# A fixed issue order by a table, and seven half-size products in every token tile from the fifth on

## The chip, the cores and the metric

The kernel runs on one core of one Trainium2 chip. The metric is the device time of one execution in microseconds (us). A core has five engines that run side by side, each through its own queue in order: TensorE (PE: matmul; PEld: its weight loads), VectorE (DVE), ScalarE (ACT), GpSimd (POOL) and SyncE (SP). SP and POOL issue the transfers here, which 16 DMA engines carry out. SBUF is the memory beside the engines; PSUM holds the sums of matmuls in eight banks.

## The reference

Two layers, the second fed by the first. Input x is 8 batches of 3008 rows of 256 numbers.

```
X  = rfft(x, axis=1)
Yr = Xr @ w_r - Xi @ w_i + b_r ;  Yi = Xr @ w_i + Xi @ w_r + b_i
Y  = soft_threshold(Yr, 0.01) + 1j * soft_threshold(Yi, 0.01)
y  = irfft(Y, n=3008, axis=1)              # 24064 rows of 256
h  = y @ w_in                              # 256 -> 2048
g  = s * relu(h)**2 + b
out = g @ w_out                            # 2048 -> 256
```

## The kernel before

**Spectral part.** 3008 = 94 x 32, and the transform is done in two stages of matmuls. Per batch: first stage (`s1_units`: matmul of x with A_t, a copy out of PSUM into u, transfer u to a DRAM buffer ud, and back as us, rows regrouped), then `s23_units`: second stage (F_t), mixing with w_r and w_i by three products (xf, W_t, W_g, the sum s), soft threshold (`shrink`: max, min, subtract on VectorE in a ring of buffers), four transfers ring to ring per step that regroup partitions, first inverse stage (T_t, copied to v), transfer v to DRAM vd and back as vs; then `s4_units`: last stage (C_t), copied to yt. The first batch runs by itself in `first_batch` with all banks; the other seven run beside the second layer of the batch ahead.

**Second layer.** The 24064 tokens make 48 token tiles (`_tile_order`): 12 "wide" ones of batches 0 and 1 (512 or 480 tokens), 30 "main" ones and 6 "tail" ones (512 or 384). Each tile has 16 slots (MC = 16 blocks of 128 of the 2048 inner columns). In a slot, `first_mm` does two matmuls of up to 512 columns into one half of a double bank psh; every second slot, relu (L879, psh to rt) and the square (L889 or L892, rt to gt) follow. In the slots of the next tile, the products gt x w_out of this tile run:

- plain (`second_mms`, L930 on): 4 groups of 16 matmuls of 256 columns into psa, two exits by VectorE (L954, psa to ost) and four stores;
- by sevens (`seven_mms`): the tile's gt as a 2 x 2 matrix of blocks, and w_out likewise, multiplied by seven products of half-size blocks instead of eight (Strassen-Winograd), 7 x 2 x 8 = 112 matmuls of 128 columns. The sums of blocks of gt are made on VectorE (`s_op`, L990, three of 1024 columns for each half of the inner columns) and, the fourth of them, by an accumulating DMA gt to gt that POOL issues (L983). The sums of w_out are made once (`make_t`). The seven results leave four banks in four groups (`leave`, L1023 and L1042: zz and ost), nine VectorE instructions in all. A bank psa is one of two; product four (n = 3) needs the bank of the first two.

Before, `seven` (L1087) picks 21 of the 48 tiles: three around the change of batch 0 to 1, the two ahead of each later batch, the first of most batches, and most of the last batch.

**What sets the order.** A plan written out by hand (`schedule`, `plan`) says in which slot each spectral unit is emitted. The engine of a copy or a square is chosen by a running sum of costs (`act_first`, `work`). The tile framework's scheduler then sets each engine's order by priorities; `urgent()` (L183) raises those of instructions that empty a bank.

Of the kernel before, what the change touches and what calls it, by code (L numbers as in the profile page):

```python
# [9 lines left out]
F16 = mybir.dt.float16  # L10
# [9 lines left out]
VSCALE = 1.0 / 64.0  # L20

# [75 lines left out]
def kernel(  # L97
# [70 lines left out]
    lean = [0.0]  # L168

    pe = {"on": False, "now": 0.0}  # L170

    def matmul(out, lhs, rhs, **how):
        if pe["on"]:
            pe["now"] += 0.0025 + int(np.prod(rhs.shape[1:])) / 2400.0
        return nc.tensor.matmul(out, lhs, rhs, **how)  # L175

    def work(engine, us):
        load[engine] = max(load[engine], pe["now"]) + us

    def act_first(ready, ta, td):  # L180
        return max(load["act"], ready) + ta <= max(load["dve"], ready) + td + lean[0]

    def urgent():  # L183

        return tc.high_priority(offset=200) if pe["on"] else nullcontext()

    def evac(dst, src, cols):
        ta, td = over["act"] + cols / 1200.0, over["dve"] + cols / 960.0
        with urgent():
            if act_first(pe["now"], ta, td):  # L190
                work("act", ta)
                return None, nc.scalar.copy(out=dst, in_=src)  # L192
            work("dve", td)
            return nc.vector.tensor_copy(out=dst, in_=src), None
# [3 lines left out]
    def mix_bank():  # L198
        return pools["m"].tile([P, 512], F32, name="psm", tag="psm")
# [10 lines left out]
    def two_banks():  # L210
        return pools["h"].tile([P, 2, 512], F32, name="psh", tag="psh")

    def one_bank():
        return fpool.tile([P, 512], F32, name="psf", tag="psf")
# [4 lines left out]
    def other_bank():  # L219
        return apool.tile([P, 512], F32, name="psa", tag="psa")  # L220
# [6 lines left out]
    def emit_load_x(b, first=None, chunks=range(N2 // XCH)):  # L227
        xv = x[b].rearrange("(n1 n2) d -> n1 (n2 d)", n2=N2)
        for c in chunks:
# [4 lines left out]
            if first is not None:  # L234
                gate = nc.gpsimd.tensor_copy(out=t[0:1, 0:1], in_=first)
# [133 lines left out]
    last_square = [None]  # L369
# [4 lines left out]
    def make_t(i):  # L374

        if not T_s:
            nc.vector.tensor_tensor(
                out=b_21, in0=bias_bc[:, P:D], in1=bias_bc[:, 0:P], op=ALU.subtract
            )
            T_s.append(x2pool.tile([P, 4, MC // 2, P], F16, name="T_s", tag="x2"))  # L380
        t = T_s[0]
        a, b, op = (
            (w_block(0, 1), w_block(0, 0), ALU.subtract),
            (t[:, 0], w_block(1, 1), ALU.subtract),
            (w_block(1, 1), w_block(0, 1), ALU.subtract),
            (w_block(1, 0), t[:, 1], ALU.add),
        )[i]
        with tc.issue_after(last_square[0].ins):
            nc.vector.tensor_tensor(out=t[:, i], in0=a, in1=b, op=op)
        work("dve", 0.61)  # L390
# [9 lines left out]
    def make_bias():  # L400
# [3 lines left out]
        nc.scalar.activation(out=bias_bc, in_=ps[:, 0:D], func=AF.Copy, scale=bb_bc)  # L404
# [3 lines left out]
    ring = []  # L408
    yts = {}
    tails = {}  # L410
# [3 lines left out]
    def first_batch():  # L414
# [121 lines left out]

        def turn(ec, n):

            ps = mix_bank() if ec == 0 else any_bank() if n < HW else one_bank()
            for j in range(4):  # L540
# [5 lines left out]
            evac(  # L546
                vs[(0, h)][:, k : k + 4, ec * P : (ec + 1) * P],
# [5 lines left out]
        def last_dft(ec, n):  # L553
# [5 lines left out]
            else:  # L559
                ps = other_bank() if n % 8 else one_bank()  # L560
            for j in range(4):
# [6 lines left out]
            evac(  # L568
                yt[:, ec, n : n + 4, :],
                ps[:, 0:384].rearrange("p (j n) -> p j n", n=96), 384,  # L570
            )

# [51 lines left out]
    def s1_units(b, more_banks=False):  # L624

        ud = dpool.tile([96, N2, D], F16, name="ud", tag="ud")
        hold = {}

        def unit(i):
# [4 lines left out]
            ps = any_bank() if more_banks else one_bank()  # L634
            matmul(
# [4 lines left out]
            evac(u[0:96, k : k + 2, :], ps[0:96, :].rearrange("p (j d) -> p j d", j=2), 512)  # L640
            if k == UCH - 2:
                n = 2 * i + 2
                nc.sync.dma_start(out=ud[:, n - UCH : n, :], in_=u[0:96])

        def take_rows(which=range(4)):
            uv = ud.rearrange("k n d -> (k n) d").rearrange("(q p) d -> p q d", p=P)
            for q in which:
                t = uspool.tile([P, 6, D], F16, name="us", tag="us")
                nc.sync.dma_start(out=t, in_=uv[:, 6 * q : 6 * q + 6, :])
                us[(b, q)] = t  # L650
# [3 lines left out]
    def s23_units(b):  # L654
# [6 lines left out]
        hold = {}  # L661

        def fwd_unit(i):
# [3 lines left out]
            t = us[(b, i // 3)]  # L667
            for j in range(2):
# [7 lines left out]
            evac(xt[:, 1:3].rearrange("p r c k -> p (r c k)"), bank, 512)  # L676
            nc.vector.tensor_tensor(out=xt[:, 0], in0=xt[:, 1], in1=xt[:, 2], op=ALU.add)  # L677
            work("dve", 0.34)
            xf[i] = xt

        def sum_unit(h):

            ps = one_bank().rearrange("p (i e) -> p i e", i=2)
# [6 lines left out]
            s = mpool.tile([P, 2, D], F32, name="s", tag="m")  # L690
            with urgent():
                nc.scalar.copy(out=s, in_=ps)
            work("act", 0.49)
            hold[h] = s

        def mix_unit(i):
            ps = one_bank().rearrange("p (r e) -> p r e", r=2)
            xt = xf.pop(i)
            for r in range(2):
# [5 lines left out]
            with urgent():  # L705
                nc.vector.tensor_tensor(  # L706
                    out=ring[0][:, i % 4], in0=ps,
                    in1=hold[i // 2][:, i % 2].unsqueeze(1).to_broadcast([P, 2, D]), op=ALU.add,
                )
            work("dve", 0.67)  # L710
# [5 lines left out]
        def shrink(i, n):  # L716
# [4 lines left out]
            nc.vector.tensor_tensor(out=m, in0=t, in1=lo, op=ALU.max)  # L721
            nc.vector.tensor_tensor(out=m, in0=m, in1=hi, op=ALU.min)
            nc.vector.tensor_tensor(out=t, in0=t, in1=m, op=ALU.subtract)
            work("dve", 0.21 + 0.8 * n)
            for k in range(i, i + n):
                z = ring[0][:, 6 + k % 6]
                for j in range(2):
                    for r in range(2):
                        o = z[64 * r : 64 * r + 64, j]
                        a = t[64 * j : 64 * j + 64, k - i, r]  # L730
                        if k < H - 2:
                            nc.sync.dma_start(out=o, in_=a)
                        else:
                            nc.vector.tensor_copy(out=o, in_=a)
                            work("dve", 0.13)
                zt[k] = z

        def inv_unit(i):
            ps = one_bank().rearrange("p (j e) -> p j e", j=2)
            z = zt.pop(i)  # L740
            for j in range(2):
# [7 lines left out]
            evac(v[:, h : h + 2, :], ps, 512)  # L749
            if i % 2 == 1:  # L750
                nc.sync.dma_start(
                    out=vd[2 * i - 2 : 2 * i + 2].rearrange("q p e -> p q e"), in_=v
                )
            if i == H - 1:
                hold["vv"] = vd.rearrange("q (k n) e -> (q k) (n e)", n=N2)
# [4 lines left out]
        def take_half(h):  # L760
            t = vspool.tile([96, HW, D], F16, name="vs", tag="vs")
            nc.sync.dma_start(
                out=t.rearrange("k n e -> k (n e)"),
                in_=hold["vv"][:, h * HW * D : (h + 1) * HW * D],
            )
            vs[(b, h)] = t
# [17 lines left out]
    def s4_units(b):  # L784
# [6 lines left out]
        def unit(g):  # L791
# [4 lines left out]
            ps = one_bank()  # L796
            for j in range(w):
# [6 lines left out]
            evac(  # L804
                yt[:, ec, n2 : n2 + w, 0:N1],
                ps[:, 0 : w * N1].rearrange("p (j n) -> p j n", n=N1), w * N1,
            )
            if g == len(groups) - 1 and b >= 2:
# [3 lines left out]
                nc.gpsimd.tensor_copy(out=tails[pr][:, :, half], in_=yt[:, :, :, 80:94])  # L812
# [22 lines left out]
    hold_h = {}  # L835

# [21 lines left out]
    def first_mm(ti, mc):  # L858
# [4 lines left out]
        ps = hold_h["ps"]  # L863
        for dc in range(DC):
# [12 lines left out]
        rt = rpool.tile([P, 2, 512], F32, name="rt", tag="rt")  # L877
        with urgent():
            nc.scalar.activation(out=rt[:, :, 0:w], in_=ps[:, :, 0:w], func=AF.Relu)  # L879
# [4 lines left out]
        rr = rt[:, :, 0:w]  # L884
        if halves(ti):
            rr = rr.rearrange("p k (i t) -> p k i t", i=2)
        work("act", 0.07 + w / 600.0)
        if act_first(pe["now"], 0.09 + w / 600.0, 0.07 + w / 480.0):
            nc.scalar.activation(out=gt, in_=rr, func=AF.Square)  # L889
            work("act", 0.09 + w / 600.0)  # L890
        else:
            last_square[0] = nc.vector.tensor_tensor(out=gt, in0=rr, in1=rr, op=ALU.mult)  # L892
            work("dve", 0.07 + w / 480.0)
    def store(tl, sub, src):
        kind, b, j, w = tl
        if kind == "wide":
# [3 lines left out]
            nc.sync.dma_start(  # L900
                out=rows[n2 : n2 + 4, lo : lo + w], in_=src[0 : 4 * w]
            )
            return
        if kind == "main":
            rows = out[b * N + 512 * j : b * N + 512 * (j + 1), :]
            rows = rows.rearrange("(n1 n2) d -> n2 n1 d", n2=N2)[8 * sub : 8 * sub + 8]
            nc.sync.dma_start(out=rows, in_=src)
# [4 lines left out]
        while i < end:  # L912
# [14 lines left out]
            nc.sync.dma_start(out=dst, in_=src[i - i0 : i - i0 + cnt])  # L927
            i += cnt

    def second_mms(ti):  # L930
# [6 lines left out]
        def mm(sub, mc):  # L937
# [3 lines left out]
            if h == 0 and mc == 0:  # L941
                hold["ps"] = sum_bank(ti).rearrange("p (h e) -> p h e", h=2)
            ps = hold["ps"]
            matmul(
# [5 lines left out]
            if mc == MC - 1 and (alone or h == 1 or sub == nsub - 1):  # L950
                k = h + 1
                ost = opool.tile([P, 2, D], F32, name="ost", tag="ost")
                with urgent():
                    nc.vector.scalar_tensor_tensor(  # L954
                        out=ost[0:size, 0:k], in0=ps[0:size, 0:k], scalar=s_bc[0:size],
# [3 lines left out]
                work("dve", 0.13 + 0.27 * k)  # L959
                for i in range(k):  # L960
                    store(tl, sub - k + 1 + i, ost[:, i, :])
# [7 lines left out]
    sums = {}  # L969

# [4 lines left out]
    def s_op(ti, n, q):  # L975

        size = 2 * sub_size(tiles[ti])
        if n == 1:
# [213 lines left out]
```

## Time and profile before

| | |
|---|---|
| median of 3 runs | 836.48 us (836.18 to 836.76) |
| the profiled execution | 837.46 us, its span 835.7 us |
| TensorE busy | 820.7 us, 7662 matmuls |
| ScalarE busy | 723.0 us |
| VectorE busy | 703.9 us |
| GpSimd busy | 86.3 us |
| HBM read and written | 53.52 and 46.66 MB |
| granted TensorE clock | 1.0 |

The span goes from the first to the last instruction. A busy time is the union of an engine's instructions. A row of a group gives the engine, the operation, output and input by the program's names, shapes and count, then busy time and the mean of one instruction. A matmul row's end is modelled and holds the drain, which the next matmul overlaps; so the distance between two starts says what one costs. In rows in order of time, merged rows (x7) go from the first start to the last end, and a bracket gives the idle time ahead and who ended it.

The token tiles start at 46.3 us (tile 0), 114.6 (tile 4), 302.2 (tile 15), 351.7 (tile 18), 405.5 (tile 21), 797.0 (tile 46) and 810.1 (tile 47).

### The profile page before, as it was taken

What the parts mean: (1) busy time and instruction counts of PE and PEld (TensorE: products, weight loads), DVE (VectorE), ACT (ScalarE), POOL (GpSimd) and SP (SyncE); (2) the same over time, 40 slices, a digit from 0 to 9 for tenths busy, and PEclk for the clock granted to TensorE, in tenths of its full rate; (3) what the DMA queues carried; (4) which work ended last, traced back from release to release, by engine and by line L of the source; (5) the groups of instructions that cost most, each with busy time, mean ns of one, the idle gap of its engine ahead of it and who ended that gap; (6) DMA issues with size and microseconds to landing.
All of it is one profiled execution on the core that took longest, in us unless ns stands there. A gap on an engine that the chain in (4) does not pass through costs nothing.

```text
span 835.7 us, 19552 instructions
## 1 busy us (share of the span) xinstructions
PE 820.7 (98%) x7662; PEld 598.5 (72%) x7662; DVE 703.9 (84%) x1104; ACT 723.0 (87%) x962; POOL 86.3 (10%) x114
## 2 busy tenths in 40 slices
PE   7999999999999999999999999999999999999997
PEld 6857767777677767777677776777767777767765
DVE  5988979978898888987889888797888988879785
ACT  5998988998899988998899988989879988788882
POOL 4550001100011001100011000100001000001000
PEclk9999999999999999999999999999999999999999
DMA  8954578346773378445773458724565233513321
GB/s 201 178 155 102 116 193 208 61 97 138 193 185 66 96 182 200 124 104 137 182 191 71 97 137 208 183 48 114 128 178 141 59 103 100 135 45 77 77 62 59
DMA packets 116670, 107.17 MB, mean 128 GB/s; under 512 B 12774, under 2 KB 100842, under 8 KB 115234
## 3 DMA queue, kind: packets, MB, share of 16 engines
q1 hardware_dynamic: 102498, 80.55, 34.0%
q0 software_dynamic: 14080, 25.37, 19.1%
q8 instruction: 60, 0.98, 0.5%
q14 instruction: 32, 0.26, 0.1%
HBM read 53.52 MB, written 46.66 MB: 120 GB/s over the span
## 4 chain that ended last, share of the span: by engine, by line
PE 78%; DVE 9%; ACT 5%; DMA 5%; issue 2%; POOL 0%; SPq 0%; DVEq 0%; POOLq 0%
PE psh L175 32%; PE psa L175 28%; PE psf L175 17%; ACT rt L879 2%; DVE gt L892 2%; DMA vd<-v 1%; DMA ring<-ring 1%; DMA x<-in_x_dram 1%; DVE ring L706 1%; DVE gt L990 1%; PE psm L175 1%; DVE ost L1023 1%; DMA vs<-vd 1%; ACT gt L889 1%; DVE s L990 1%
## 5 line engine op out<-in xcount | busy, mean ns | idle before, releaser
L879 ACT ACTIVATE rt<-psh 128x1024 f32<-128x1024 f32 (+2 forms) x384 | 386.9, 1009 | 56.0 <-PE psh L175 54.0
L175 PEld LDWEIGHTS <-gt 128*128 128x128 f16 (+1 forms) x3696 | 304.9, 101 | 167.2 <-issue 0.5
L175 PE MATMUL psh<-yt,w_in 128*128 128x512 f16 (+1 forms) x1344 | 396.7, 378 | 0.1
L892 DVE TENSOR_TENSOR gt<-rt 128x1024 f16<-128x1024 f32 (+2 forms) x239 | 286.0, 1201 | 81.3 <-ACT rt L879 80.6
L175 PE MATMUL psa<-w_out_t,gt 128*128 128x256 f16 (+3 forms) x2448 | 310.3, 253 | 0.0
L175 PEld LDWEIGHTS <-w_in 128*128 128x128 f16 x1536 | 136.5, 98 | 25.4 <-issue 2.9
L889 ACT ACTIVATE gt<-rt 128x1024 f16<-128x1024 f32 (+2 forms) x145 | 150.8, 1040 | 3.4
L175 PE MATMUL psa<-T_s,gt 128*128 128x128 f16 (+1 forms) x944 | 79.4, 219 | 0.0
L983 POOL DMA_DIRECT2D gt<-gt x42 | 38.0, 905 | 325.7 <-PE psh L175 87.3
L192 ACT CAST u<-psf 96x512 f16<-96x512 f32 x96 | 55.7, 582 | 9.1 <-PE psf L175 8.4
L706 DVE TENSOR_TENSOR ring<-psf,s 128x512 f16<-128x512 f32 x84 | 57.4, 684 | 4.1 <-PE psf L175 3.1
L192 ACT CAST v<-psf 128x512 f16<-128x512 f32 x79 | 45.8, 583 | 14.0 <-PE psf L175 13.5
L175 PE MATMUL psh<-tail,w_in 128*128 128x512 f16 (+1 forms) x192 | 52.1, 352 | 0.0
L239 POOL DMA_DIRECT2D x<-in_x_dram x36 | 19.2, 538 | 315.6 <-PE psf L175 314.4
L175 PEld LDWEIGHTS <-xf 128*128 128x128 f16 x504 | 46.7, 98 | 5.8 <-DVE xf L677 0.4
L175 PE MATMUL psf<-W_g,xf 128*128 128x256 f16 x336 | 50.4, 272 | 0.0
L192 ACT CAST yt<-psf 128x470 f16<-128x470 f32 (+2 forms) x84 | 43.1, 535 | 3.4 <-PE psf L175 2.2
L1023 DVE SCALAR_TENSOR_TENSOR ost<-psa,s_bc,zz 128x256 f32<-128x256 f32 (+1 forms) x80 | 34.7, 477 | 7.9 <-PE psa L175 6.4
L954 DVE SCALAR_TENSOR_TENSOR ost<-psa,s_bc,bias_bc 128x512 f32<-128x512 f32 (+2 forms) x51 | 37.1, 727 | 4.8 <-PE psa L175 2.6
L192 ACT CAST xf<-psf 128x512 f16<-128x512 f32 x64 | 37.5, 586 | 3.8 <-PE psf L175 3.7
L175 PE MATMUL psf<-x,A_t 94*96 94x512 f16 x102 | 39.0, 382 | 1.0 <-ACT yt L192 0.3
L175 PE MATMUL psf<-C_t,vs 96*128 96x94 f16 (+1 forms) x484 | 38.0, 205 | 0.1
(118 smaller groups left out, 797.0 us busy)
## 6 DMA issues: line engine op xcount, KB each, us to landing
out_dram<-ost SPq DMA_DIRECT2D x152, 128.0 KB
ud<-u SPq DMA_DIRECT2D x56, 192.0 KB
us<-ud SPq DMA_DIRECT2D x28, 384.0 KB
vd<-v SPq DMA_DIRECT2D x42, 256.0 KB
vs<-vd SPq DMA_DIRECT2D x14, 768.0 KB
x<-in_x_dram POOLq DMA_DIRECT2D x28, 376.0 KB, 6.3
gt<-gt POOLq DMA_DIRECT2D x38, 256.0 KB, 4.2
ring<-ring SPq DMA_DIRECT2D x280, 32.0 KB
```

The lines of the kernel that those rows point to most:

```text
L175: return nc.tensor.matmul(out, lhs, rhs, **how)
L192: return None, nc.scalar.copy(out=dst, in_=src)
L239: nc.gpsimd.dma_start(out=t[0:N1, i * w : (i + 1) * w], in_=xv[:, c * XCH * D + i * w : c * XCH * D + (i + 1) * w],)
L706: nc.vector.tensor_tensor(out=ring[0][:, i % 4], in0=ps, in1=hold[i // 2][:, i % 2].unsqueeze(1).to_broadcast([P, 2, D]), op=ALU.add,)
L879: nc.scalar.activation(out=rt[:, :, 0:w], in_=ps[:, :, 0:w], func=AF.Relu)
L889: nc.scalar.activation(out=gt, in_=rr, func=AF.Square)
L892: last_square[0] = nc.vector.tensor_tensor(out=gt, in0=rr, in1=rr, op=ALU.mult)
L954: nc.vector.scalar_tensor_tensor(out=ost[0:size, 0:k], in0=ps[0:size, 0:k], scalar=s_bc[0:size], in1=bias_bc[0:size].unsqueeze(1).to_broad ...
L983: nc.gpsimd.dma_start(out=a12, in_=a11, accum_op=ALU.add)
L990: nc.vector.tensor_tensor(out=out, in0=a, in1=b, op=op)
L1023: nc.vector.scalar_tensor_tensor(out=out, in0=of, scalar=s_bc[0:size], in1=other, op0=ALU.mult, op1=ALU.add)
```

## The change

- Every token tile from tile 4 to tile 45 that has 512 or 480 tokens is done by seven products: 39 tiles instead of 21.
- After the first batch, all instructions of ScalarE, VectorE, SP and POOL are recorded as pieces (`later`) and issued in a fixed order with a fixed engine, by a table of base-36 numbers (`TURNS`): piece k is issued at place k + delay, on the engine that the table names, as soon as TensorE's program reaches it (`pump`, called ahead of each matmul). The framework's own scheduling is switched off for all five engines (`manual_schedule`).
- Copies out of PSUM, relus, squares and the copy of s may go to either engine; relu gets a VectorE form.
- Two ring transfers become one where two steps are shrunk together; the load of the fourth chunk of x is planned some slots earlier; the output and rt buffers are three fixed ones used in turn.
- Asserts (`need`, `begin`) at build time, no instructions: every piece is issued behind those that it needs.

```diff
     def seven(ti):
-        if ti >= len(tiles) - 2 or not halves(ti):
-            return False
-        firsts = [mark[b] // MC for b in range(2, B)]
-        return (
-            ti >= firsts[-1] or 4 <= ti < 7 or any(m - 2 <= ti < m for m in firsts)
-            or late(ti)
-        )
+        return 4 <= ti < len(tiles) - 2 and halves(ti)
...
+    def plan_turns():
+        at = [divmod(int(TURNS[k : k + 2], 36), 4) for k in range(0, len(TURNS), 2)]
+        queue.extend(
+            (k, ("act", "dve", "sp", "pool")[at[k][1]])
+            for k in sorted(range(len(at)), key=lambda k: k + at[k][0])
+        )
+
+    def begin(op, engine):
+        assert engine in op.cost and all(n.gone for n in op.needs)
+        op.gone = True
+        op.emit(engine)
+
+    def pump():
+        while queue and queue[0][0] < len(pieces):
+            k, engine = queue.pop(0)
+            begin(pieces[k], engine)
...
     def matmul(out, lhs, rhs, **how):
-        if pe["on"]:
-            pe["now"] += 0.0025 + int(np.prod(rhs.shape[1:])) / 2400.0
+        pump()
         return nc.tensor.matmul(out, lhs, rhs, **how)
...
+        def relu(e):
+            if e == "act":
+                nc.scalar.activation(out=rt, in_=ps[:, :, 0:w], func=AF.Relu)
+            else:
+                nc.vector.tensor_scalar(
+                    out=rt, in0=ps[:, :, 0:w], scalar1=0.0, scalar2=None, op0=ALU.max
+                )
...
+        first = later(
+            relu, {"act": 0.065 + w / 600.0, "dve": 0.065 + w / 480.0},
+            needs=squares[-len(rts) :][:1] if len(squares) >= len(rts) else [], frees=ps,
+        )
...
-        first = ((0, 1, 0), (1, 3, 0)) if late(ti) else ()
-        for at, n, q in (
-            *first, (2, 2, 0), (2, 1, 1), (2, 4, 0), (3, 3, 1), (4, 2, 1), (5, 4, 1)
-        ):
-            at += alone and at > 3
-            slots[at].append(lambda n=n, q=q: s_op(ti, n, q))
+        slots[0].insert(0, lambda: own_sums(ti, 1))
+        for at, q in ((2, 0), (4 + alone, 1)):
+            slots[at].append(lambda q=q: s_op(ti, 2, q))
...
-            for c, at in enumerate((10, 14, 26, 54)):
+            free_at = 37 + 4 * (mark[b] - s1 - 50) // 16
+            for c, at in enumerate((10, 14, 26, free_at)):
...
+    osts = [opool.tile([P, 2, D], F32, name="ost", tag="ost") for _ in range(3)]
+    rts = [rpool.tile([P, 2, 512], F32, name="rt", tag="rt") for _ in range(3)]
+    ctx.enter_context(tc.manual_schedule(engines={
+        mybir.EngineType.PE, mybir.EngineType.Activation, mybir.EngineType.DVE,
+        mybir.EngineType.SP, mybir.EngineType.Pool,
+    }))
```

## The prediction, made before the changed kernel ran

> **What bounds the kernel now.** I read the page first, parts 1 and 4, then the stretches of each token tile, the waits of TensorE, and the rows in order of time at three places.
>
> ```profile
> span 835.7 us, 19552 instructions
> PE 820.7 (98%) x7662; PEld 598.5 (72%) x7662; DVE 703.9 (84%) x1104; ACT 723.0 (87%) x962; POOL 86.3 (10%) x114
> PE 78%; DVE 9%; ACT 5%; DMA 5%; issue 2%; POOL 0%; SPq 0%; DVEq 0%; POOLq 0%
> ```
>
> TensorE is the bound: it idles 15 us of 835.7. Of this, 5.4 lie in the first 46.3 us and 4.4 in the last 25.6 us, both outside the change; 5.2 lie in the token tiles between (PE busy 758.61 of 763.80). So time can be won by less TensorE work, and by at most about 5 us of idle time besides. A busy matmul row holds a drain that the next one overlaps, so true stalls are somewhat longer than this idle time.
>
> The price of a matmul is its distance to the next, not its duration. Two rows in order of time, late in the run, then two stretches of one token tile each:
>
> ```profile
> 797.38 0.55 PE L175 MATMUL psf<-w_out_t,gt 128*128 128x128 f16 x7
> 810.54 0.60 PE L175 MATMUL psf<-w_out_t,gt 128*128 128x256 f16 x4
> ...
> 797.00:810.10 13.10, 13.10 (x146) 9.32 (x144) 12.48 (x17) 10.62 (x11) 1.71 (x2) 1.00 0.30 61
> 810.11:824.00 13.89, 13.89 (x99) 9.40 (x97) 10.01 (x11) 9.60 (x11) 0.00 (x0) 1.00 0.19 58
> ```
>
> The columns of the last two are stretch, its length, then busy time and count of PE, PEld, DVE, ACT, POOL, clock, DMA share. Seven half-size matmuls take 0.55 us, the last lasting 0.219: (0.55-0.219)/6 = 0.055 us each. Four full ones: (0.60-0.272)/3 = 0.109. The first stretch runs 32 wide matmuls and one tile's seven products, the second the same 32 and one tile's plain second product.
>
> **The change, part by part.** *TensorE.* A plain tile has 4 x 16 = 64 matmuls of 256 columns: 64 x 0.109 = 6.98 us. Seven products are 7 x 2 x 8 = 112 matmuls of 128: 112 x 0.0557 = 6.24. That is 0.74 less per tile; the two stretches say 0.79. Tiles by sevens go from 21 to 39 of 48, 18 more (16 of 512 tokens, two of 480 with the same columns): **-13.4 us**. The built order has 18 x 48 = 864 more matmuls, so the change does do this. TensorE's order is now that of the program: from tile 3 on it is the same but for two matmuls in tile 12; five first-stage matmuls of batch 1 that ran in gaps ahead of tile 0 now stand inside it: 0 to 5 x 0.22 = +1.1 us, taken as 0, since the gaps ahead of it wait for copies that these five also waited for.
>
> *VectorE and ScalarE.* Each added tile brings VectorE six sums (687 ns, rows of L990) and nine exits (seven of 477, one of 413, one of 746 ns) for two exits of 748: 4.12+4.50-1.50 = 7.1 us, 128 us for 18. Against that the built order moves 121 squares from VectorE (239 to 118) to ScalarE, 39 relus to VectorE and 80 copies to VectorE. ScalarE: squares +126.9, relus -39.0, copies -46.1, together +42, 723 to 765 us. VectorE: -145.9 squares, +46.3 relus (no row; 1.22 us each, as the square of the same 1024 floats takes; at the least 0.69 as a sum of 1024 halves, 21 us less in all; at the most 1.37 as two PSUM casts of 512, 6 us more), +53.8 copies, +128: 786 us. As rows of one line overlap (three exits in 1.26 us are 0.39 apart, not 0.477), 231 more instructions cost some 0.085 less each: 766. Both engines stay below 822 as a whole, at 93 to 96%. They lie beside TensorE, and cost nothing as long as nothing waits.
>
> The dense tiles decide that. Three consecutive tiles that are plain now, with spectral work beside them:
>
> ```profile
> 351.70:405.50 53.80, 53.15 (x452) 38.06 (x450) 45.36 (x75) 48.96 (x65) 2.80 (x4) 1.00 0.51 122
> ```
>
> VectorE plus ScalarE: 94.3 us in 2 x 53.8. Two and a half added tiles (the first exits already run there) at 6.0 (7.1 less 13 x 0.085) are +15, less about 3 for squares on the cheaper engine: 106 against 2 x 51.6 = 103. Without the overlapped 0.09 of each of about 175 instructions it is 91. So between 88% and 103% of the two engines; at the upper end each such group lacks (106-103)/2 = 1.6 us, and there are six: 0 to +10 us. I take +2, nearer the lower end, because in the neighbouring tile of 17.5 us ScalarE is busy 16.67 with TensorE's idle time all from one VectorE wait (next).
>
> *The fixed order.* The only regular wait of TensorE in these tiles is this:
>
> ```profile
> PE psa L175 <- DVE ost L1023: 3.5, 7, 0.8
> PEld L175 <- DVE ost L1023: 5.1, 9, 0.9
> ...
> 358.04 0.48 DVE L1023 SCALAR_TENSOR_TENSOR zz<-psa,s_bc,bias_bc 128x256 f32<-128x256 f32 x1
> 358.43 0.68 DVE L722 TENSOR_TENSOR ring<-ring,high 128x1024 f16<-128x1024 f16 x1
> 359.03 0.48 DVE L1023 SCALAR_TENSOR_TENSOR ost<-psa,s_bc,zz 128x256 f32<-128x256 f32 x1
> 359.57 0.23 PE L175 MATMUL psa<-T_s,s 128*128 128x128 f16 x1 [0.65 <-DVE ost L1023]
> ```
>
> The fourth product wants the bank of the first two; VectorE empties the first, does a shrink, and only then empties the second. In the built order of before something stands between these two exits in 16 of 21 tiles; in the changed one in 9 of 39, and in two of those nine only the short sum of zz. I take -4 of the 5.1 us (bounds: -5 by all idle time of the middle, to +2, the 9 tiles at 0.8 less the 5.1 of now). What is late next is the relu and the square, which then queue behind the exits.
>
> *Transfers.* 36 more accumulating DMAs. Two of them in the stretch 797 to 810 kept the software queue at 23.1% of 13.1 us, 1.5 us each of all 16 engines: +54 us, DMA share 53% to about 60%. POOL pays 36 x 0.9 us, beside 749 us of idle. Ring moves are halved in number where two were merged (280 to 160 issues on SP), bytes the same. On SP's queue a store now stands where the table puts it, ahead of which a ring move or a write of v may wait; VectorE's exits wait for stores by three buffers as before. It matters where DMA has no slack:
>
> ```profile
> 306.15 7.06 DMA vd<-v
> 313.21 0.02 issue
> 313.23 7.57 DMA vs<-vd
> 320.80 0.04 issue
> 320.84 0.59 PE psf L175 x10
> ```
>
> This chain, of batch 3, lands just when TensorE needs it; DMA is 0.85 busy there. The changed kernel puts two accumulating DMAs (3 us) into it, and takes one load of x (chunk 3, ten slots earlier) out. In the other batches vs lands 3.3 to 6.8 us ahead of use. So 0 to +3 us at one place; I take +1.
>
> *Sum.* Profiled run 837.46 (span 835.7): -13.4 +2 -4 +1 = -14.4, 823.1. The median of the runs shown, 836.48, is 0.98 below the profiled run: **822 us**. Bounds: best -13.4 -5 - some hidden stalls (5) = 812; worst -13.4 +10 +2 +3 +1 = 839.
>
> **The rivals.** *A, slower: the banks pass on late in most tiles.* Place: the fourth product in slot 7 of each seven-product tile, which needs two exits from an in-order VectorE that is over 90% full. Price: 0.8 us per tile, as now. All 39 tiles: 31-5 = +26 us, with -13.4 a time of 849. It decides from 13.4/0.8 = 17 further tiles on. For it: it happens in seven to nine of 21 tiles with VectorE at 84%. Against it: in 30 of 39 tiles nothing stands between the exits. 0.12.
>
> *B, the engines become the bound in the dense tiles, with DMA late too:* +10 and +3, with the exits no better: 836 to 837, or half of it 830. For it the 103% above and DMA shares of 0.82 to 0.90 at the batch changes; against it that the overlap brings the load down to 91 of 103. 0.13, mostly still faster.
>
> *C, weights become the bound.* A half-size matmul has 0.056 us for a weight load whose row lasts 0.098; if loads did not overlap, a tile would take 112 x 0.098 = 10.98 instead of 6.98, +72 us for 18, 908. The stretch of 797 to 810 excludes it: 144 loads in 13.10 us without idle time. 0.01. The Trainium skill, page "TensorE: Matmul & The Clock Gate", section "Back-to-back issue gap", gives 81 ns per matmul of 128 columns in streams of load and matmul; by that a tile would take 9.1 us, and the change would cost 18 x 2.1 = 38 us, near 873. The trace does not agree: 0.055 us in such a stream.
>
> *Forecast:* TensorE's 13.4 us come through, stalls stay about what they are. 0.74.
>
> **How the numbers follow.** Range: 812 (all stalls gone) to 834 (B by three quarters); it leaves out A and the rest of B. Faster by over 0.2% (under 834.8; less cannot be told from no change): 0.74 and 0.09 of B, 0.83. Within: 0.04. Slower: 0.12 of A and C's 0.01, 0.13.
>
> **What would show it.** Half-size matmuls still 0.056 us apart and the added tiles 0.75 us shorter: the first term. VectorE and ScalarE both 755 to 790 us busy: the second. Waits of TensorE for VectorE's exits below 2 us in all: the third. Batch 3's wait for vs under 3 us: the fourth. I am wrong if TensorE's idle time between 46 and 800 us exceeds 15 us, above all as many short waits for relu or exits, or if accumulating DMAs land later than the last product needs them.

## The result, and the profile after

| | before | after |
|---|---|---|
| median | 836.62 us (836.18 to 837.41, 4 runs) | 893.01 us (892.21 to 894.42, 4 runs) |
| ratio, 95% interval | | 1.0675 [1.0656, 1.0693] |
| profiled execution, span | 837.46, 835.7 us | 892.21, 890.4 us |
| sum of TensorE's normal distances | 808.9 us | 796.3 us |
| what TensorE's starts are late beyond it | 21.3 us | 87.7 us |

The kernel became 6.75% slower. The last two rows are worked out from the trace: each matmul is given the median distance from its start to the next one's for its shape, and the rest is lateness (how finely the shapes are told apart moves each figure by up to 4 us, and the differences between the two kernels by less than 1). TensorE's work is 12.6 us shorter, its lateness 66.4 us more. Medians and ratios here and below leave out one run (898 us, of experiment 2) that lay more than 1.5% above the fastest of its kernel.

The page of after, parts 1 and 2:

```profile
span 890.4 us, 21353 instructions
...
PE 827.7 (93%) x8526; PEld 609.0 (68%) x8526; DVE 770.2 (86%) x1335; ACT 757.6 (85%) x965; POOL 116.7 (13%) x148
...
PEclk9999999999899898999889999899999999999999
DMA  8963556746747467555566565845665544623322
```

VectorE and ScalarE are as busy as predicted (766 and 765), yet only 86 and 85% of the longer span. The clock row, all nines before, has eights. TensorE's waits in after (total us, times, longest):

```profile
PE psf L241 <- DMA vs<-vd: 17.9, 4, 5.8
PE psa L241 <- DMA gt<-gt: 14.4, 7, 4.8
PE psf L241 <- DMA ring<-ring: 12.6, 4, 5.8
...
PE psh L241 <- DVE rt L1133: 1.0, 2, 0.8
```

Three kinds of transfer hold TensorE: v's way back as vs, the accumulating transfers that make the fourth sum of gt, and the ring moves. Before, only one such wait was there:

```profile
PE psf L175 <- DMA ring<-ring: 0.9, 1, 0.9
```

The waits for VectorE's exits (ost) are no longer in the list of after. Eleven stops of more than 1.5 us make up 44.3 us of the lateness. One of them, in the rows of TensorE in order of time, and then the stretches around it (length, busy time and count of the five engines, clock, DMA share, GB/s):

```profile
452.47 0.50 PE L241 MATMUL psa<-w_out_t,gt 128*128 128x128 f16 x6
457.78 0.29 PE L241 MATMUL psa<-w_out_t,gt 128*128 128x128 f16 x1 [4.82 <-DMA gt<-gt]
```

```profile
440.00:455.10 15.10, 12.97 (x136) 8.95 (x133) 14.06 (x20) 11.27 (x14) 1.69 (x2) 1.00 0.72 176
455.10:457.10 2.00, 0.00 (x0) 0.00 (x0) 0.00 (x0) 0.00 (x0) 0.00 (x0) 0.99 1.02 267
457.10:460.60 3.50, 2.82 (x13) 1.59 (x14) 0.47 (x2) 1.70 (x3) 0.00 (x0) 0.50 0.08 30
460.60:462.60 2.00, 2.00 (x15) 1.44 (x14) 1.21 (x4) 0.96 (x1) 0.00 (x0) 0.50 0.00 0
```

For two microseconds no engine computes and all 16 DMA engines are full. When TensorE starts again, its granted clock is 0.50: in the last stretch it is busy throughout, with nothing to wait for, at half speed. Eight stops (2.3 to 6.0 us) are followed by such a stretch of 3.4 or 6.8 us, 47.8 us in all, some of it still inside the stop; the matmuls in them are 16.7 us late beside the stops (for each no more than 1.1 times its own distance is counted). So 44.3 + 16.7 = 61.0 of the 87.7 us are stops and clock.

The write of v is late for a second reason. SP's issues and then VectorE's rows at the change to batch 3:

```profile
327.29 2.71 SPq L1168 DMA_DIRECT2D out_dram<-ost  x4
330.10 0.40 SPq L972 DMA_DIRECT2D vd<-v  x1
330.60 1.62 SPq L804 DMA_DIRECT2D ud<-u  x2
332.27 0.92 SPq L972 DMA_DIRECT2D vd<-v  x1
338.03 0.30 SPq L988 DMA_DIRECT2D vs<-vd  x1
```

```profile
324.06 0.68 DVE L304 CAST v<-psf 128x512 f16<-128x512 f32 x1
324.66 0.47 DVE L1331 SCALAR_TENSOR_TENSOR ost<-psa,s_bc,zz 128x256 f32<-128x256 f32 x1
325.05 0.68 DVE L304 CAST v<-psf 128x512 f16<-128x512 f32 x1
325.65 1.21 DVE L1144 TENSOR_TENSOR gt<-rt 128x1024 f16<-128x1024 f32 x1
326.78 0.48 DVE L1331 SCALAR_TENSOR_TENSOR ost<-psa,s_bc,zz 128x256 f32<-128x256 f32 x1
```

The piece of v that VectorE finished at 324.74 is written at 330.10: the table has four stores ahead of it, the first waits for the exit that ends at 327.26, and the four take 0.68 us of issue each. The same write left SP 0.03 us behind its copy in the median before, and 4.04 us in after (largest 9.9). TensorE then stands 5.25 us for vs at 342.

### The profile page after: what moved, and what is told of

It is laid out like the page before. It is cut to its first block, busy times and chain, and to the rows that moved or that the text cites. A ratio compares the mean times of both kernels' runs of the same rounds, so it can differ in the third digit from the quotient of the medians.

```text
span 890.4 us, 21353 instructions
## 1 busy us (share of the span) xinstructions
PE 827.7 (93%) x8526; PEld 609.0 (68%) x8526; DVE 770.2 (86%) x1335; ACT 757.6 (85%) x965; POOL 116.7 (13%) x148
## 3 DMA queue, kind: packets, MB, share of 16 engines
q0 software_dynamic: 20032, 34.78, 23.9%
## 5 line engine op out<-in xcount | busy, mean ns | idle before, releaser
L241 PEld LDWEIGHTS <-gt 128*128 128x128 f16 (+1 forms) x4272 | 315.0, 102 | 174.4 <-DMA gt<-gt 15.8
L1142 ACT ACTIVATE gt<-rt 128x1024 f16<-128x1024 f32 (+2 forms) x266 | 274.7, 1043 | 4.3 <-DVE rt L1133 1.4
L241 PE MATMUL psa<-w_out_t,gt 128*128 128x128 f16 (+3 forms) x2160 | 215.7, 233 | 16.2 <-DMA gt<-gt 14.4
L241 PE MATMUL psa<-T_s,gt 128*128 128x128 f16 (+1 forms) x1808 | 152.4, 220 | 0.0
L1144 DVE TENSOR_TENSOR gt<-rt 128x1024 f16<-128x1024 f32 (+2 forms) x118 | 141.5, 1208 | 9.9 <-ACT rt L1131 9.4
L1331 DVE SCALAR_TENSOR_TENSOR zz<-psa,s_bc,zz 128x256 f32<-128x256 f32 (+3 forms) x109 | 61.3, 563 | 1.4
L1274 DVE TENSOR_TENSOR gt<-gt,s 128x1024 f16<-128x1024 f16 (+1 forms) x78 | 53.0, 681 | 6.1 <-PE psa L241 5.0
L1133 DVE TENSOR_SCALAR rt<-psh 128x1024 f32<-128x1024 f32 (+2 forms) x39 | 46.2, 1187 | 12.1 <-PE psh L241 10.1
L1274 DVE TENSOR_TENSOR s<-gt 128x1024 f16<-128x1024 f16 (+1 forms) x78 | 53.8, 690 | 1.1
L1274 DVE TENSOR_TENSOR gt<-gt 128x1024 f16<-128x1024 f16 (+1 forms) x78 | 54.1, 695 | 0.7
L241 PE MATMUL psa<-T_s,s 128*128 128x128 f16 (+1 forms) x560 | 54.4, 220 | 0.3
L304 ACT CAST u<-psf 96x512 f16<-96x512 f32 x77 | 44.3, 579 | 10.1 <-PE psf L241 9.7
```

The costliest lines, as they stand in the source:

```text
L304: (nc.scalar.copy if e == "act" else nc.vector.tensor_copy)(out=dst, in_=src)
L1133: nc.vector.tensor_scalar(out=rt, in0=ps[:, :, 0:w], scalar1=0.0, scalar2=None, op0=ALU.max)
L1274: nc.vector.tensor_tensor(out=out, in0=a, in1=b, op=op)
L1331: nc.vector.scalar_tensor_tensor(out=out, in0=of, scalar=s_bc[0:size], in1=other, op0=ALU.mult, op1=ALU.add)
```

## The experiments

Three theories were held against each other. **Q**: SP's fixed order holds back the writes of v and u. **D**: the added accumulating transfers fill the DMA engines where a batch changes, and land late. **E**: VectorE and ScalarE are full, and the transfers only show it. All runs are in rounds beside the kernel before; a ratio has its 95% interval.

**1. SP's order, alone and with POOL's.** In the call of `manual_schedule`:

```diff
-        mybir.EngineType.SP, mybir.EngineType.Pool,
+        mybir.EngineType.Pool,
```

> The changed kernel, with SyncE's queue alone left to the framework's scheduler; every other engine's order stays as in the changed kernel, so only the order in which SP issues stores, ring moves, writes of u and v and loads of us and vs differs. Theory Q (the table's order of SP's queue: a write of v or a ring move stands behind stores whose exit is not done, and is issued 4 us late at the median, and TensorE stalls behind vs and ring): the lag of the v writes behind their copies falls from 4.0 to under 1 us, TensorE's waits for vs and ring from 30 us to under 6, the clock is back at 1.0, and the time is 825 to 855. Theory D (36 more accumulating transfers load the DMA engines, and everything lands late): the transfers are all still there, so at least 880. Theory E (VectorE's and ScalarE's fixed orders are late): at least 880, since these orders are untouched.

885.3 us, 1.0571 [1.0528, 1.0613], 8 us less than after. Writes of v leave 0.04 us behind their copies again, and the waits for vs go. But the time does not follow, since others take their place. TensorE's waits:

```profile
PE psa L241 <- DMA gt<-gt: 27.2, 11, 5.3
PE psf L241 <- DMA ring<-ring: 10.9, 6, 4.1
```

The waits for the fourth sum double (14.4 to 27.2 us). From issue to landing the worst accumulating transfer takes 8.0 us before, 10.2 in after, 12.5 here: v and u now leave on time, into the same DMA engines. From issue to landing of that worst transfer these engines are 0.92 busy in after (447.5 to 457.7 us) and 0.91 here (326.8 to 339.3). Q alone falls. With POOL's order free too:

> As the run with SP's queue free, and POOL's queue free too (accumulating transfers, loads of x). Theory Q: SP's queue is what counts, so within 6 us of the run with SP alone free, unless waits for gt are left there, which this then takes away. Theory D and E: at least 880.

884.9 us, 1.0543 [1.0496, 1.059], the same: with SP's queue free, POOL's order plays no part.

**2. The 39 tiles by sevens without any of the rest** (kernel before):

```diff
-        if ti >= len(tiles) - 2 or not halves(ti):
-            return False
-        firsts = [mark[b] // MC for b in range(2, B)]
-        return (
-            ti >= firsts[-1] or 4 <= ti < 7 or any(m - 2 <= ti < m for m in firsts)
-            or late(ti)
-        )
+        return 4 <= ti < len(tiles) - 2 and halves(ti)
```

> The kernel before, unchanged but for the choice of tiles: 39 by seven products instead of 21; its own scheduler sets the order. Theory Q: the transfers of the sums are no burden, so TensorE's 13 us come through less some waits for VectorE, which the old planner loads more: 822 to 845. Theory D: the same 36 transfers as in the changed kernel, so 870 or more with waits for gt and vs. Theory E in the form that the work of 39 tiles is too much for VectorE and ScalarE in any order: 860 or more with waits for relus and exits.

886.5 us (877 to 887, three runs), 1.0551 [1.0486, 1.0617]. Most of the loss comes with the added sevens, under the old scheduler too. Q falls; D and E had both forecast this.

**3. No fixed order at all** (the call of `manual_schedule` taken out of after):

> The changed kernel's pieces, buffers and engines by the table, but all five orders left to the framework's scheduler, with no raised priority for instructions that empty a bank. Theory Q: most of the loss is gone as in the run with SP free; what the compute engines' fixed orders are worth is the difference to that run, 0 to 25 us slower than it. Theory E: this one is clearly faster than the run with SP alone free. Theory D: at least 880.

893.2 us, 1.0674 [1.0617, 1.0731]. With both late causes in place, the table as a whole neither gains nor loses against this free order, which also lacks the raised priorities that the kernel before has.

**4. The fourth sums left out, in all 39 tiles and in six** (the tile three ahead of each batch change, 12 transfers):

```diff
-                nc.gpsimd.dma_start(out=a12, in_=a11, accum_op=ALU.add)
+                pass
```

```diff
+                if not any(ti == mark[c] // MC - 3 for c in range(2, B)):
+                    nc.gpsimd.dma_start(out=a12, in_=a11, accum_op=ALU.add)
```

> The changed kernel without any of its 78 accumulating transfers: the fourth sum of each half is left out, so products that use it work on the wrong block; every engine's order is otherwise that of the changed kernel. Theory D (the accumulating transfers overfill the DMA engines at the batch changes; ring moves, vs and the sums themselves land late, and each stop of several us also halves the clock for a while): TensorE's waits for gt are gone, those for ring and vs below 10 us in all, time 820 to 845. Theory Q (SP's order) says that waits for vs and ring stay, 870 or more, since SP is untouched. Theory E (compute engines late): 860 or more.

> The changed kernel with the fourth sums left out in six tiles alone, those whose products run in the second tile ahead of a new batch (9, 14, 20, 26, 32, 38): 12 of 78 transfers fewer. Theory D in its narrow form (it is the batch change alone, where vs, us, v and u move): most of the loss comes back, 835 to 855. Theory D in its wide form (36 more transfers cost wherever they stand): a sixth to a third, 870 to 885. Theory Q and E: 885 or more.

861.5 us, 1.0263 [1.0225, 1.0302], and 873.4 us, 1.0418 [1.0397, 1.0439]. All transfers are worth 31.5 us, and the 12 in six tiles 19.6 of these. No forecast fits whole: 861.5 us lies above D's 845, below Q's 870, and in E's "860 or more"; 873.4 lies in the range of D's wide form, yet 12 of 78 transfers bring 19.6 of 31.5 us, so the batch changes count for more than the number. D holds for this part of the loss. A transfer left out takes its load and TensorE's wait for its landing away together, so these runs do not part the two. What is left without any of them is Q's wait, TensorE's largest there:

```profile
PE psf L241 <- DMA vs<-vd: 16.7, 6, 5.1
PE psf L241 <- DMA ring<-ring: 2.8, 2, 2.6
```

**5. The fourth sum on GpSimd, in after and in the kernel of 2:**

```diff
-                nc.gpsimd.dma_start(out=a12, in_=a11, accum_op=ALU.add)
+                nc.gpsimd.tensor_tensor(out=a12, in0=a12, in1=a11, op=ALU.add)
```

> The changed kernel with the fourth sum made by a GpSimd addition in place of the accumulating transfer, at the same place of POOL's queue; nothing left out. Theory D: near the run without fourth sums, 820 to 850, if an addition of 1024 on GpSimd takes under 3 us and does not hold VectorE up; with VectorE held by two readers of SBUF, up to 880 and VectorE's sums longer than 0.69 us. Theory Q: 870 or more with waits for vs. Theory E: 870 or more.

> The kernel before with 39 tiles by seven products, its own scheduler, and the fourth sums by GpSimd additions instead of transfers. Theory D: the 887 of the same kernel with transfers falls to 825 to 850. Theory E (the work of 39 tiles on VectorE and ScalarE): stays above 865, with waits for relus and exits.

936.6 us, 1.1176 [1.1147, 1.1206], and 964.3 us, 1.1495 [1.1476, 1.1514]: worse, and slower than the forecasts of D. The run meant to free the DMA engines says little on them, as it slows VectorE. The group of the sum in the first of the two, and one of VectorE's own sums (busy us, mean ns), which takes 695 ns in after:

```profile
L1288 POOL TENSOR_TENSOR gt<-gt 128x1024 f16<-128x1024 f16 (+1 forms) x78 | 177.3, 2275 | 569.4 <-DVE gt L1274 379.6
...
L1274 DVE TENSOR_TENSOR gt<-gt 128x1024 f16<-128x1024 f16 (+1 forms) x78 | 71.6, 919 | 0.8
```

VectorE's busy time goes from 770.2 to 863.9 us with the same instructions.

**6. Both causes away: no fourth sums, SP's order free:**

> The changed kernel without its 78 accumulating transfers (fourth sums left out) and with SP's queue left to the framework. Theory D+Q (both hold a share: the accumulating transfers some 32 us, the order of SP's queue the waits for vs of 17 us that stayed without them, and the clock behind them): 832 to 845, waits for vs under 4 us. Theory D alone (the rest is VectorE's and ScalarE's fixed order): stays within 5 us of 861.

836.4 us, 0.9989 [0.9972, 1.0006]. The two causes together take 56.6 of the 893.0 us, alone 31.5 and 7.7, or 39.2: each hides part of the other. The merged ring moves, the fixed buffers, the earlier load of x and the relus on VectorE are all in this kernel, so they are no part of the 56.6. The runs are of different rounds, in which the kernel before took 836.6 to 838.4 us; by the ratios 31.5 would be 34.5, 7.7 would be 8.7, and the step from 861.5 to 836.4 would be 23 and not 25, so such differences hold to some 3 us. TensorE's lateness falls to 32.3 us, against 21.3 before. Where each late start is put down to what released it, leaving out the first 114.6 and the last 39 us, 14.1 us of it end with VectorE (5.8 before) and 3.9 with a transfer of SP (0.4 before).

**7. Nearest versions that leave nothing out.** The six tiles' fourth sums by VectorE with SP free (after); and the kernel before with 33 sevens, the same six tiles staying plain:

> The changed kernel, SP's queue free, and the twelve fourth sums of the six tiles two ahead of a new batch added by VectorE in place of a transfer; nothing left out. Theory D+Q: 838 to 862, below both single steps (885 with SP free, 873 with the six left out). If the two losses are one and the same, it stays at 870 or more.

> The kernel before with its own scheduler and 33 tiles by seven products: the 39 less the six whose products run in the second tile ahead of a new batch. Theory D in its narrow form (only transfers that fall on the batch change cost): 825 to 842, at least 40 us below the 887 of all 39. In its wide form (24 more transfers cost anywhere): 850 to 870. Theory E: 860 or more, with waits for exits and relus.

858.3 us, 1.0242 [1.0201, 1.0284], and 853.3 us, 1.0185 [1.0158, 1.0212]. The first is where D and Q together put it. Six plain tiles bring the old order 33 us, 886.5 to 853.3, less than the 40 that D's narrow form asked for; 853 lies in the range of its wide form.

**8. The old order with 39 sevens, the 36 added transfers left out:**

> The kernel before with its own scheduler and 39 tiles by seven products, the 36 accumulating transfers of the 18 added tiles left out (their fourth sums are missing). Theory D: 822 to 842, so that the 36 transfers alone are worth 45 to 65 us of the 887. Theory E (VectorE's and ScalarE's added work): 855 or more.

858.7 us, 1.0236 [1.0185, 1.0286]. Here too the added transfers are worth 28 us, and something else remains, as E forecast (855 or more). In the trace, counted as in 6, it is VectorE above all: 20.4 us of late starts end with VectorE, 9.4 with a transfer of SP, 8.3 with ScalarE (5.8, 0.4 and 1.6 before).

**9. What remains.** All fourth sums on VectorE, SP free, nothing left out (the diff of 5 with `nc.vector`); and the fourth sums left out under the framework's order:

> All 78 fourth sums move from accumulating transfers to VectorE, SP's order free; nothing is left out. The same kernel without these sums ran in 836.4 us with VectorE busy about 770. 78 sums at 0.69 us are 54 us, so VectorE would be busy some 820 us. If the rest of the loss (836 against the 823 that TensorE's gain would give) is many short waits for VectorE, which is near its limit in the dense tiles, the time rises by a good part of the 54 us: 860 to 885. If the transfers and SP's order were the whole of it, and VectorE has room, it stays at 836 to 845.

> The changed kernel with the framework's order on all engines, and the 78 accumulating transfers left out (so the fourth sums are not made). With the transfers this order gave 893.2 us, and SP alone freed gave 885.3. If the fixed order of VectorE and ScalarE is worth something once the transfers are gone, this runs slower than the 836.4 us of the fixed order with SP free: 845 to 860, near the 858.7 of the old order without the added transfers. If that order is worth nothing and the transfers are all, it gives 834 to 840.

868.8 us, 1.0378 [1.036, 1.0396], and 876.9 us, 1.0479 [1.0432, 1.0526]. The first puts 41.7 us more on VectorE than the kernel of 6 (766.8 to 808.5) and gets 32.4 us longer, inside the forecast for that case: VectorE had almost no room left. Counted as in 6, the late starts that end with VectorE go from 14.1 to 44.1 us. Tiles 15 to 20 in the kernel before, in that of 6, and in this one:

```profile
302.20:405.50 103.30, 102.29 (x951) 73.20 (x949) 88.63 (x138) 94.23 (x126) 8.77 (x12) 1.00 0.61 147
```

```profile
304.00:405.40 101.40, 100.33 (x1094) 73.28 (x1093) 99.34 (x175) 97.04 (x123) 2.92 (x5) 1.00 0.49 127
```

```profile
310.90:417.40 106.50, 101.84 (x1094) 73.51 (x1092) 105.25 (x185) 98.18 (x123) 3.78 (x5) 1.00 0.47 121
```

VectorE, the third busy time, is at 86%, 98% and 99% of its stretch. The chain that ended last can be followed back for a little over half of the span only. What there is of it runs more over TensorE in the kernel of 6 (first line), more over VectorE in this one (second line), whose granted clock is 1.00 in these tiles:

```profile
PE 37%; DVE 15%; issue 2%; DMA 1%; ACT 1%; DVEq 0%; SPq 0%; ACTq 0%
DVE 26%; PE 22%; issue 4%; ACT 2%; DMA 1%; SPq 0%; DVEq 0%; ACTq 0%
```

So E holds for most of what is left in the kernel of 6, once the DMA engines are no longer the limit. The second run lies outside both forecasts (845 to 860, 834 to 840). It says that the table's order on the other engines is worth 876.9 - 836.4 = 40 us against the framework's order without raised priorities, once the transfers and SP's order are out of the way; with the transfers in place it is worth 8 (893.2 with no fixed order, 885.3 with SP's alone free). TensorE waits for vs there (four stops, 16.9 us in all), though the writes of v leave 0.03 us behind their copies at the median; what makes vs late there stays open.

No version here beats the kernel before: the one that comes level leaves out a sum.

## Why the prediction was wrong, point by point

Predicted 822 us, range 812 to 834; measured 893. Of its terms:

- *TensorE, -13.4.* Right: -12.6, and seven half-size products of after lie as close as before (0.55 us, (0.55-0.219)/6 = 0.055 each).

```profile
340.89 0.55 PE L241 MATMUL psa<-w_out_t,gt 128*128 128x128 f16 x7
```

- *VectorE and ScalarE, 766 and 765 us busy.* Right: 770.2 and 757.6. The relu on VectorE takes 1187 ns (taken as 1.22 us). "I take +2, nearer the lower end" of 0 to +10 was too low. Without the fourth sums and with SP free, 836.4 us is 12.4 above 836.6 - 12.6 = 824.0, with VectorE at 98% in the dense tiles; the upper end was nearer. That VectorE has no room there is measured (experiment 9). In the trace of that kernel late starts that end with VectorE are 8.3 us more than before, those that end with a transfer of SP 3.5 more, so most of the 12.4 us is VectorE's doing, not all.
- *The fixed order of exits, -4.* Right as to the waits: those for ost (3.5 us before) are not in after's list, and rival A did not come. But other waits for VectorE took their place (for v, gt, rt and ring): in all they are 8.1 us in after against 5.3 before, so the 4 us were not won.
- *Transfers, +1.* **This step failed**: "So 0 to +3 us at one place; I take +1." Measured: 31.5 us by the accumulating transfers and 25.1 by SP's order behind them (861.5 to 836.4). The load itself was right: by the pages the software queue took 19.1% of 835.7 us before and 23.9% of 890.4 in after, 53 us more, where 54 were forecast. The chain of batch 3 was rightly named as the place with no slack, but its wait for vs is 5.25 us, not under 3. What the prediction took as slack, "in the other batches vs lands 3.3 to 6.8 us ahead of use", was slack under the old SP order, and a median lag of 4 us uses it up in several batches at once. I priced the added transfers by their share of the DMA engines as a mean (53 to 60%) and by one stretch of 3 us. Their landing, not their share, is what the last product waits for, and at the batch changes, where the share was already 0.82 to 0.90, it went up to 10.2 us in after and 12.5 with SP free. The six tiles whose sums fall there had been plain before. The prediction's own sign of being wrong, "if accumulating DMAs land later than the last product needs them", is what came.
- *"On SP's queue a store now stands where the table puts it, ahead of which a ring move or a write of v may wait."* This mechanism was seen but given no price. It is the other half of the loss, with the sides changed: the write of v waits behind the store.
- *Nothing in the sum* stood for the half clock behind a stop, 16.7 us of after, which the two numbers above contain.
- Rival B ("the engines become the bound in the dense tiles, with DMA late too", 830 to 837) named full engines and late transfers together, with DMA priced at +3; it has nothing on SP's order or the clock.

The sum, mended: 836.6 - 12.6 + 12.4 (full VectorE for the most part) + 25.1 (SP's order) + 31.5 (transfers) = 893.0. It closes by how its terms were taken; that 25.1 and 31.5 overlap is seen in 7.7 for SP's order alone. The trace of after gives an account that does not close by construction. Counted as in experiment 6, its 74.5 us of lateness (8.5 before) end with ring moves and vs for 32.4, with fourth sums for 15.8, with VectorE for 9.4 (5.8 before), and for 16.6 us with nothing, which is the half clock.

Two sums of the prediction are a little off, without effect: its best case adds up to 813, and (106-103)/2 is 1.5.

## What to carry to other kernels

Price an added transfer by its landing time in the very stretch where it falls, with that stretch's DMA share and the moment its reader needs it; the added load was forecast rightly here, and its mean share of the span did not show the loss. A fixed order on a queue that issues transfers makes each of them wait for the data of those ahead of it, so for each one ask what the instruction ahead waits for. When one of two late causes is taken away and the time hardly moves, take both before calling either harmless.

## What the runs showed of the hardware

- **The clock halves behind short stops.** Of eleven stops over 1.5 us in after, eight (2.3 to 6.0 us) were followed by 3.4 or 6.8 us at 0.50; those of 1.6, 2.0 and 2.4 us were not. The Trainium skill, page "TensorE: Matmul & The Clock Gate", section "HAM oscillation — how this bites in real kernels", gives as the rule no idle gaps over about 3.4 us. The stop of 2.3 us at 170.5 is below that, and the clock still fell at 173.8. In after the eight stretches begin on one grid of steps of 3.41 us: their starts lie 19, 16, 15, 26, 7, 32 and 60 steps apart. In the step just ahead of each, TensorE idled 62 to 100% of the time; the stop of 2.4 us at 216.2 fell across two steps and took 51% of one, that of 2.0 us at 669.9 took 53%. So where a stop falls on this grid counts beside its length. The line is not sharp: in the second run of experiment 5 one step with 52% of idle time was followed by the half clock, and one with 54% was not.
- **A sum on GpSimd slows VectorE's two-input sums** from 695 to 919 ns in the mean. In the first run of experiment 5 the 22 sums gt<-gt of 1024 columns that a GpSimd addition overlapped took 1473 ns, the other 50 took 707; the exits that read one operand from PSUM took 483 ns with such an overlap (24 of them) and 477 without. The Trainium skill, page "SBUF — State Buffer", section "Who interferes with whom", says that a VectorE instruction with two SBUF inputs contends with a GpSimd instruction that reads SBUF; the trace agrees.
- **An accumulating transfer of 256 KB** lands in 3.3 us at best in after and in the run with SP free, and at worst in 10.2 and 12.5 us, with the DMA engines 0.92 and 0.91 busy meanwhile.
